# An attention and feed-forward kernel on one core: another order of instructions on four engines, and two PSUM banks shared by transposes and attention result

## The chip, the core and the metric

The kernel runs on 1 core of one Trainium2 chip. The metric is the device time of one execution in microseconds (us); shown is the median of several runs. One execution was also profiled, and all rows of the profile come from that one.

The engines are named as the profile names them: PE multiplies matrices (PEld is its loading of the stationary operand), DVE, ACT and POOL work on elements, SP issues DMAs. Each engine takes its instructions in the order in which they stand in its queue, and an instruction that waits holds up those behind it on the same engine. A line number such as L203 is that of the kernel before; in the changed kernel the same statements of the functions stand up to 7 lines lower.

## The reference

```python
# q, k, v: (8, 8, 576, 64) float32, tau = 0.02; w_in (512, 2048), w_out (2048, 512) float64
scores = 0.125 * np.matmul(q, k.transpose(0, 1, 3, 2))
thresh = np.max(scores, axis=-1, keepdims=True) - tau
scores = np.where(scores >= thresh, scores, -1000000000.0)
scores = scores - np.max(scores, axis=-1, keepdims=True)
attn = np.exp(scores)
attn = attn / (np.sum(attn, axis=-1, keepdims=True) + 1e-09)
x = np.matmul(attn, v)          # (8, 8, 576, 64)
x = x.transpose(0, 2, 1, 3).reshape(4608, 512)
h = x @ w_in
r = np.maximum(h, 0.0)
out = (r * r) @ w_out           # (4608, 512)
```

## The kernel before, in words

Two heads are taken together (32 pairs). Their 576 queries are cut into four blocks of 128 and a rest of 64; the rests of the two heads share a block. Work goes by *steps*, one block of a pair each, 160 in all (numbered from 0). The first four pairs are visited twice, first blocks 0, 1, 2 (steps 0 to 11), then blocks 3 and 4 (steps 12 to 19), so that the first chunk of the feed-forward part is ready early; from step 20 on each pair has its five blocks in one visit. Everything is issued by one loop over the steps, and its order of statements is the order in every queue: no scheduler moves anything.

A step does the following.

- `scores`: PE multiplies one block of queries with all keys (L179) into PSUM tiles s0 and s1, one for each head, two banks each and only one copy of them. DVE takes the row maximum (L183) and three small numbers from it: the bias b (L184), the threshold (L185) and z (L188). ACT takes the exponentials (L191).
- `threshold`: DVE sets to zero what lies under the threshold and sums the rest (L203); after it s0 and s1 are free for the next step's scores. Then the reciprocal of the sum (L205, L206), and POOL divides (L208).
- `turn`, for the step before, in three parts: PE transposes a third of the weights w (L220; L224, L230 and L231 for the block of rests) into a PSUM bank "tr", and ACT copies it to SBUF as wT (L221, L227, L232, L233). "tr" is one bank, so a part can't start before the copy of the part before has read it. Before step 13 (`early()`), parts 1 and 2 use the two "mm" banks, which the feed-forward part doesn't need yet.
- `mix`, two steps after the blocks 2 and 4 of a pair: PE multiplies wT with v (L247) into the bank "x", and ACT copies the result (L250) to xT.
- `fill`: what is waiting of the feed-forward part, in four portions between the parts of `turn`, by given costs of each piece of PE work. `mlp_in` multiplies xT with w_in (L263), ACT takes the relu (L267), POOL squares it (L269); `mlp_out` multiplies with w_out (L279), ACT copies (L283), SP stores. Chunks of 384 tokens are released at fixed steps: chunk 0 at step 13, the next at step 39.
- `load_qk`, `load_v`: SP loads the next pair. `prep`, at the end of the second step of a visit: DVE lays out qT and kT of the next pair (L154), POOL copies the pieces qmid (L161) and the first columns of kT (L157), which the next visit's first scores read.
- `round_weights`: the weights come as float64 and are rounded to float32 in 32 pieces, four of them loaded ahead. Stage 0 is two conversions on ACT (L113, L114), stage 1 three bit operations on DVE (L116, L117, L119), stage 2 a multiply and an addition on POOL (L121, L122). Their tile cv has two copies. A piece's stages 0, 1 and 2 stand after the scores, before the threshold, and at the end of its step. Pieces per step come from `FEW, MORE = 0.5, 1.6`: one in steps 1, 3, 5, 7, 9, 11 and 12; then 2, 1, 2, 2, 1, 2, 1 in steps 13 to 19; 2, 2, 1, 2, 1, 2, 2, 1 in steps 20 to 27; and the last in step 28.

PSUM's eight banks: s0 and s1 take four, "mm" two, "tr" one, "x" one.

Of the kernel before, what the change touches and what calls it, by code (L numbers as in the profile page):

```python
# [9 lines left out]
FP32 = mybir.dt.float32  # L10
U32 = mybir.dt.uint32
AF = mybir.ActivationFunctionType
ALU = mybir.AluOpType
# [6 lines left out]
def kernel(  # L20
# [75 lines left out]
    def load_weights(i):  # L96
        nc.sync.dma_start(out=weight_area(i).bitcast(mybir.dt.int64), in_=weight_piece(i)[0])
# [3 lines left out]
    def round_weights(i, stage):  # L101

        words = weight_area(i).bitcast(U32).rearrange("p (n w) -> p n w", w=2)
        lo, hi = words[:, :, 0], words[:, :, 1]
        if stage == 0:
            rounding[i] = pool.tile([P, 3, WP], FP32, tag="cv", name="cv")
        t, e, d = (rounding[i][:, x, :] for x in range(3))  # L110
        tu, eu = t.bitcast(U32), e.bitcast(U32)
        if stage == 0:
            nc.scalar.activation(out=e, in_=hi.bitcast(FP32), func=AF.Copy, scale=2.0 ** -112)  # L113
            nc.scalar.activation(out=d, in_=lo, func=AF.Copy, scale=2.0 ** -52)  # L114
        elif stage == 1:
            nc.vector.tensor_scalar(out=tu, in0=hi, scalar1=0x80000000, scalar2=None, op0=ALU.bitwise_and)  # L116
            nc.vector.scalar_tensor_tensor(out=tu, in0=eu, scalar=3, in1=tu, op0=ALU.logical_shift_left,  # L117
                                           op1=ALU.bitwise_or)
            nc.vector.tensor_scalar(out=eu, in0=tu, scalar1=0xFF800000, scalar2=None, op0=ALU.bitwise_and)  # L119
        else:  # L120
            nc.gpsimd.tensor_tensor(out=d, in0=d, in1=e, op=ALU.mult)  # L121
            nc.gpsimd.tensor_tensor(out=weight_piece(i)[1], in0=t, in1=d, op=ALU.add)  # L122

    loaded, ready = {}, {}
# [40 lines left out]
    def scores(vis, i):  # L165

        qT, kT = ready[vis]
        n = 2 if i < NBLK else 1
        sc = [psum.tile([P, 2, 512], FP32, tag=f"s{u}", name=f"s{u}") for u in range(n)]
        halves = [(half, u) for half in range(2) for u in range(n)]  # L170
        if early():
            halves.sort(key=lambda x: x[1])
        for half, u in halves:
            if i < NBLK:
                rows, lhsT = slice(u * D, (u + 1) * D), qT[u * D:(u + 1) * D, i * P:(i + 1) * P]
            else:
                rows, lhsT = slice(0, P), qmid[vis % 2]
            at = (0 if u else REST) + half * HALF
            nc.tensor.matmul(sc[u][:, half, 0:HALF], lhsT, kT[rows, at:at + HALF], start=True, stop=True)  # L179
        st = pool.tile([P, 7, 2], FP32, tag="st", name="st", bufs=4)  # L180
        mx, bias, thr, z = (st[:, j, 0:n] for j in range(4))
        for u in range(n):
            nc.vector.tensor_reduce(out=mx[:, u:u + 1], in_=sc[u][:, :, 0:HALF], axis=AX.XY, op=ALU.max)  # L183
        nc.vector.tensor_scalar(out=bias, in0=mx, scalar1=-SCALE, scalar2=None, op0=ALU.mult)  # L184
        nc.vector.tensor_scalar(out=thr, in0=mx, scalar1=ntau8, scalar2=None, op0=ALU.add)  # L185


        nc.vector.tensor_tensor(out=z, in0=thr, in1=mx, op=ALU.is_gt)  # L188
        w = pool.tile([P, n, S], FP32, tag="w", name="w", bufs=3)
        for u in range(n):  # L190
            nc.scalar.activation(out=w[:, u, :].rearrange("p (h k) -> p h k", h=2), in_=sc[u][:, :, 0:HALF],  # L191
                                 func=AF.Exp, bias=bias[:, u:u + 1], scale=SCALE)
        weights[vis, i] = w, sc, st

    def threshold(vis, i):


        w, sc, st = weights[vis, i]
        n = len(sc)
        mx, bias, thr, z, sm, den, rcp = (st[:, j, 0:n] for j in range(7))  # L200
        for u in range(n):
            wu = w[:, u, :].rearrange("p (h k) -> p h k", h=2)
            nc.vector.scalar_tensor_tensor(out=wu, in0=sc[u][:, :, 0:HALF], scalar=thr[:, u:u + 1], in1=wu,  # L203
                                           op0=ALU.is_ge, op1=ALU.mult, accum_out=sm[:, u:u + 1])
        nc.vector.scalar_tensor_tensor(out=den, in0=z, scalar=float(S), in1=sm, op0=ALU.mult, op1=ALU.add)  # L205
        nc.vector.reciprocal(rcp, den)  # L206
        for u in range(n):
            nc.gpsimd.tensor_scalar(out=w[:, u, :], in0=w[:, u, :], scalar1=z[:, u:u + 1],  # L208
                                    scalar2=rcp[:, u:u + 1], op0=ALU.add, op1=ALU.mult)

    def turn(vis, i, part):

        w = weights[vis, i][0]
        tag = "mm" if early() and part else "tr"
        ps = psum.tile([P, 4, P], FP32, tag=tag, name="w_ps", bufs=2 if tag == "mm" else 1)
        if i < NBLK:
            cols = slice(i * P, (i + 1) * P)
            for n in range(3):
                c = 3 * part + n
                nc.tensor.transpose(ps[:, n, :], w.rearrange("p u k -> p (u k)")[:, c * P:(c + 1) * P], ident)  # L220
            nc.scalar.copy(wT[:, 3 * part:3 * part + 3, cols], ps[:, 0:3, :])  # L221
        elif part == 0:
            for c in range(NBLK):
                nc.tensor.transpose(ps[:, c, :], w[:, 0, c * P:(c + 1) * P], ident)  # L224
            for u in range(2):
                at = u * (NBLK + 1)
                nc.scalar.copy(wT[:, at:at + NBLK, NBLK * P:S], ps[:, :, u * D:(u + 1) * D])  # L227
        elif part == 1:

            nc.tensor.transpose(ps[0:REST, 0, :], w[:, 0, S - REST:S], ident)  # L230
# [6 lines left out]
    def mix(n, cols):  # L237

        b, pr = divmod(visits[n][0], HP)
        if b // 2 not in xTs:  # L240
            xTs[b // 2] = pool.tile([P, NMC, 2 * S], FP32, tag="xT", name="xT")
        nq = cols.stop - cols.start
        ps = psum.tile([P, TCH], FP32, tag="x", name="x_ps")
        for c in range(NBLK + 1):
            for u in range(2):
                cw = NBLK if c == NBLK else u * (NBLK + 1) + c
                nc.tensor.matmul(ps[u * D:(u + 1) * D, 0:nq], vs[n % 2][:, u * (NBLK + 1) + c, :], wT[:, cw, cols],  # L247
                                 start=(c == 0), stop=(c == NBLK))
        to = (b % 2) * S + cols.start
        nc.scalar.copy(xTs[b // 2][:, pr, to:to + nq], ps[:, 0:nq])  # L250
# [64 lines left out]
    def early():  # L315
        return state["step"] < min(chunk_at)
# [20 lines left out]
            fn(*what)  # L337


    FEW, MORE = 0.5, 1.6  # L340
    at_once = min(chunk_at) - 2
    rounded = [min(n_pieces, int(FEW * (min(s, at_once) + 1) + MORE * max(s - at_once, 0))) for s in range(NST)]
    load_qk(0)
    load_v(0)
    for i in range(RAW):
        load_weights(i)
    for part in range(2):
        prep(0, part)
    for s in range(NST + 3):
        state["step"] = s  # L350
        now = range(rounded[s - 1] if s else 0, rounded[s]) if s < NST else ()
        if s < NST:
            n, i = steps[s]
            at = visits[n][1].index(i)
            if at == 0 and n + 1 < len(visits):
# [18 lines left out]
        if s < NST:  # L374
# [42 lines left out]
```

## Time and profile before

| | us |
|---|---|
| median of 3 runs | 1743.04 (1740.65 to 1743.19) |
| the profiled execution, its own time | 1741.98 |
| its span, first to last instruction | 1740.2 |
| PE busy | 1586.0 (91%) |
| DVE, ACT, POOL busy | 697.3, 565.8, 496.5 |
| granted PE clock, mean over the span | 0.968 |
| longest waits of PE: for the transposes' copies (L221), the thresholds (L203), the rests' copies (L227), kT's columns (L157) | 64.8, 30.4, 24.5, 16.2 |

Rows of the profile read like this. In a timeline: start, duration, engine, line, operation, out<-in, shape, how many such instructions in a row, and in brackets how long the engine stood idle before it and who released it. In a table of waits: engine and line that waited, for whom; total us, how often, the longest. In groups of instructions: busy time, mean ns of one, idle time before. A matmul of float32 shows as two records, so the eight records of one step's scores are four matmuls.

### The profile page before, as it was taken

Reading aid. Unit: us, or ns where it says so; the run is one execution under the profiler, and the core shown is the slowest. Engines: PE = TensorE matmul, PEld = TensorE weight load, DVE = VectorE, ACT = ScalarE, POOL = GpSimd, SP = SyncE. Lnnn points to the kernel's source line nnn. Section 1 sums busy time; section 2 is a strip of 40 time slices with the busy share of each in tenths; the row PEclk is TensorE's granted clock in tenths of the full one; section 3 lists DMA queues with packets and bytes.
Section 4 is the critical chain, followed back from the end, with each engine's and each line's share of the span. In section 5 each row is a group of like instructions: output and inputs, shape, how many; then the busy total and the mean of one; then the engine's idle time right before and its main releaser. Section 6 shows DMA issues by size and latency. Waiting matters only on the chain.

```text
span 1740.2 us, 18567 instructions
## 1 busy us (share of the span) xinstructions
PE 1586.0 (91%) x6464; PEld 853.6 (49%) x6464; DVE 697.3 (40%) x1833; ACT 565.8 (33%) x1157; POOL 496.5 (29%) x655
## 2 busy tenths in 40 slices
PE   5766677889999999999999999999999999999999
PEld 3433333445545545545545545545445545545453
DVE  5755676444334343434334333434333334430000
ACT  3443443333323333323323333333323323322010
POOL 3445465123213213223213213214223213213030
PEclk8778888999999999999999999999999999999999
DMA  5334331021021010111011011021012011000000
GB/s 127 78 90 111 91 86 45 7 53 21 6 49 26 7 41 12 25 35 21 21 31 30 6 36 18 15 43 23 15 31 35 1 33 27 0 26 1 13 6 18
DMA packets 224189, 59.28 MB, mean 34 GB/s; under 512 B 215392, under 2 KB 215392, under 8 KB 224096
## 3 DMA queue, kind: packets, MB, share of 16 engines
q1 hardware_dynamic: 224064, 58.10, 14.9%
q8 instruction: 51, 0.84, 0.2%
q14 instruction: 42, 0.34, 0.1%
q0 software_dynamic: 32, 0.00, 0.0%
HBM read 48.63 MB, written 9.44 MB: 33 GB/s over the span
## 4 chain that ended last, share of the span: by engine, by line
PE 79%; DVE 8%; ACT 7%; POOL 3%; issue 2%; SPq 0%; DMA 0%; ACTq 0%; DVEq 0%; POOLq 0%
PE o L279 27%; PE h L263 24%; PE s L179 11%; PE x_ps L247 9%; PE w_ps L220 7%; DVE st L183 5%; ACT w L191 3%; ACT wT L221 1%; DVE w L203 1%; POOL cv L121 1%; DVE cv L117 1%; DVE st L184 1%; ACT cv L113 1%; ACT wT L227 1%; POOL w_in_sb L122 1%
## 5 line engine op out<-in xcount | busy, mean ns | idle before, releaser
L263 PE MATMUL h<-xT,w_in_sb 128*128 128x384 f32 x1536 | 556.4, 498 | 0.0
L279 PE MATMUL o<-w_out_sb,g 128*128 128x512 f32 x1152 | 544.2, 602 | 0.0
L183 DVE TENSOR_REDUCE st<-s 128x1 f32<-128x576 f32 x288 | 207.2, 753 | 733.4 <-PE s L179 733.3
L208 POOL TENSOR_SCALAR w<-w,st 128x576 f32<-128x576 f32 x288 | 233.9, 821 | 663.6 <-DVE st L206 600.4
L191 ACT ACTIVATE w<-s,st 128x576 f32<-128x576 f32 x288 | 199.2, 737 | 552.0 <-DVE st L184 444.4
L263 PEld LDWEIGHTS h<-xT,w_in_sb 128*128 128x128 f32 x1536 | 274.7, 193 | 166.0 <-issue 35.3
L269 POOL TENSOR_TENSOR g<-r 128x384 f32<-128x384 f32 x192 | 159.2, 829 | 525.9 <-ACT r L267 525.7
L279 PEld LDWEIGHTS o<-w_out_sb,g 128*128 128x128 f32 x1152 | 202.2, 192 | 190.4 <-issue 189.1
L221 ACT COPY wT<-w_ps 128x384 f32<-128x384 f32 x384 | 181.4, 480 | 246.5 <-PE w_ps L220 246.3
L220 PEld LDWEIGHTS w_ps<-ident,w 128*128 128x128 f32 x1152 | 148.5, 146 | 221.5 <-issue 96.6
L220 PE MATMUL w_ps<-ident,w 128*128 128x128 f32 x1152 | 197.6, 286 | 65.2 <-ACT wT L221 64.8
L203 DVE SCALAR_TENSOR_TENSOR w<-s,st,w 128x576 f32<-128x576 f32 x288 | 225.0, 814 | 79.6 <-ACT w L191 79.6
L179 PE MATMUL s<-kT,qT 64*128 64x288 f32 x1024 | 184.6, 459 | 56.9 <-DVE w L203 27.4
L179 PEld LDWEIGHTS s<-kT,qT 64*128 64x128 f32 x1024 | 104.5, 200 | 146.1 <-issue 94.9
L247 PE MATMUL x_ps<-wT,vs 128*64 128x192 f32 (+1 forms) x1280 | 174.7, 421 | 0.0
L267 ACT ACTIVATE r<-h 128x384 f32<-128x384 f32 x192 | 94.4, 492 | 181.1 <-PE h L263 172.1
L247 PEld LDWEIGHTS x_ps<-wT,vs 128*64 128x64 f32 x1280 | 87.9, 140 | 81.2 <-issue 76.0
L283 ACT COPY osb<-o 128x512 f32<-128x512 f32 x36 | 21.1, 586 | 85.3 <-PE o L279 83.5
L250 ACT COPY xT<-x_ps 128x384 f32<-128x384 f32 (+1 forms) x64 | 25.4, 397 | 51.4 <-PE x_ps L247 51.4
L179 PE MATMUL s<-kT,qmid 128*128 128x288 f32 x128 | 38.4, 425 | 3.1 <-DVE w L203 3.1
L121 POOL TENSOR_TENSOR cv<-cv 128x512 f32<-128x512 f32 x32 | 40.5, 1267 | 0.0
L188 DVE TENSOR_TENSOR st<-st 128x2 f32<-128x2 f32 (+1 forms) x160 | 38.1, 238 | 5.5
(37 smaller groups left out, 505.4 us busy)
## 6 DMA issues: line engine op xcount, KB each, us to landing
ql<-in_q_dram SPq DMA_DIRECT2D x144, 72.0 KB, 2.5
kl<-in_k_dram SPq DMA_DIRECT2D x144, 72.0 KB, 2.6
vs<-in_v_dram SPq DMA_DIRECT2D x72, 128.0 KB, 2.4
out_dram<-osb SPq DMA_DIRECT2D x36, 256.0 KB, 2.1
area<-in_moe_w_in_dram SPq DMA_DIRECT2D x16, 512.0 KB, 3.9
area<-in_moe_w_out_dram SPq DMA_DIRECT2D x16, 512.0 KB, 3.6
vs<-in_v_dram SPq DMA_DIRECT2D x72, 16.0 KB, 2.2
ntau<-in_tau_dram POOLq DMA_DIRECT2D x1, 0.5 KB, 3.3
```

Of the source, the lines that this page charges most:

```text
L179: nc.tensor.matmul(sc[u][:, half, 0:HALF], lhsT, kT[rows, at:at + HALF], start=True, stop=True)
L183: nc.vector.tensor_reduce(out=mx[:, u:u + 1], in_=sc[u][:, :, 0:HALF], axis=AX.XY, op=ALU.max)
L191: nc.scalar.activation(out=w[:, u, :].rearrange("p (h k) -> p h k", h=2), in_=sc[u][:, :, 0:HALF], func=AF.Exp, bias=bias[:, u:u + 1], sca ...
L203: nc.vector.scalar_tensor_tensor(out=wu, in0=sc[u][:, :, 0:HALF], scalar=thr[:, u:u + 1], in1=wu, op0=ALU.is_ge, op1=ALU.mult, accum_out=s ...
L208: nc.gpsimd.tensor_scalar(out=w[:, u, :], in0=w[:, u, :], scalar1=z[:, u:u + 1], scalar2=rcp[:, u:u + 1], op0=ALU.add, op1=ALU.mult)
L220: nc.tensor.transpose(ps[:, n, :], w.rearrange("p u k -> p (u k)")[:, c * P:(c + 1) * P], ident)
L221: nc.scalar.copy(wT[:, 3 * part:3 * part + 3, cols], ps[:, 0:3, :])
L247: nc.tensor.matmul(ps[u * D:(u + 1) * D, 0:nq], vs[n % 2][:, u * (NBLK + 1) + c, :], wT[:, cw, cols], start=(c == 0), stop=(c == NBLK))
L263: nc.tensor.matmul(h, w_in_sb[:, c, f * P:(f + 1) * P], xT[:, c, at:at + TCH], start=(c == 0), stop=(c == NMC - 1))
L267: nc.scalar.activation(out=r, in_=h, func=AF.Relu)
L269: nc.gpsimd.tensor_tensor(out=gs[j, f], in0=r, in1=r, op=ALU.mult)
L279: nc.tensor.matmul(o, gs[j, f][:, t * P:(t + 1) * P], w_out_sb[:, f, :], start=(f == 0), stop=(f == NFT - 1))
```

## The change

- The pieces to be rounded are set by hand. Steps 0 to 11 have one piece, except for the second step of each visit, which has `prep`; steps 12 to 19 have one each, steps 20 to 27 two each.
- Rounding has four stages, the multiply (2) and the addition (3) on POOL now apart. The first piece's conversions stand ahead of the scores' part of a step (on ACT: ahead of the exponentials), its bit operations right behind the maximum and its small numbers, its multiply ahead of the division, its addition at the step's end. A second piece has all its stages at the end of the step.
- `exponents` and `divide` are functions of their own. In steps with a piece, and in the early ones, the exponentials stand where they stood; in all others they stand behind the copy of the first third of `turn`. `threshold` moves from behind part 1 to behind part 0, the division stands behind part 1.
- `prep` moves from the end of the second step of a visit to right behind its maximum, ahead of the threshold.
- "tr" and "x" are replaced by "tx" with two banks, which transposes and mix take in turn. Early, only part 1 still uses "mm".

```diff
+        elif stage == 2:
+            nc.gpsimd.tensor_tensor(out=d, in0=d, in1=e, op=ALU.mult)
         else:
-            nc.gpsimd.tensor_tensor(out=d, in0=d, in1=e, op=ALU.mult)
             nc.gpsimd.tensor_tensor(out=weight_piece(i)[1], in0=t, in1=d, op=ALU.add)
...
-        tag = "mm" if early() and part else "tr"
-        ps = psum.tile([P, 4, P], FP32, tag=tag, name="w_ps", bufs=2 if tag == "mm" else 1)
+        ps = psum.tile([P, 4, P], FP32, tag="mm" if early() and part == 1 else "tx", name="w_ps", bufs=2)
...
-        ps = psum.tile([P, TCH], FP32, tag="x", name="x_ps")
+        ps = psum.tile([P, TCH], FP32, tag="tx", name="x_ps", bufs=2)
...
+    for s, (n, i) in enumerate(steps):
+        if s <= min(chunk_at) - 2:
+            x = int(visits[n][1].index(i) != 1)
+        else:
+            x = 1 if n < 2 * HP else 2
...
+            if now:
+                round_weights(now[0], 0)
             scores(n, i)
-        for p in now:
-            round_weights(p, 0)
+            if now or early():
+                exponents(n, i)
+            if now:
+                round_weights(now[0], 1)
+                round_weights(now[0], 2)
+            if at == 1 and more:
+                prep(n + 1, 0)
+                prep(n + 1, 1)
...
             if 0 < s <= NST:
                 turn(*steps[s - 1], part)
-            if part == 1 and s < NST:
-                for p in now:
-                    round_weights(p, 1)
+            if on and part == 0:
+                if not (now or early()):
+                    exponents(n, i)
                 threshold(n, i)
+            if on and part == 1:
+                divide(n, i)
             fill(quarter)
-        if s < NST:
-            for p in now:
-                round_weights(p, 2)
-                if p + RAW < n_pieces:
-                    load_weights(p + RAW)
-            if n + 1 < len(visits):
-                if at == 1:
-                    prep(n + 1, 0)
-                    prep(n + 1, 1)
-                if at == len(visits[n][1]) - 1:
-                    load_v(n + 1)
+        if on:
+            if now:
+                end_rounding(now[0])
+            for p in now[1:]:
+                for stage in range(3):
+                    round_weights(p, stage)
+                end_rounding(p)
+            if more and at == len(visits[n][1]) - 1:
+                load_v(n + 1)
```

The order of PE's instructions is the same in both kernels. On POOL, in step 15 (the last block of a pair, whose next pair is laid out), before: the division, two pieces of weights, qmid and kT, a square, and the division of step 16.

```order
L208 TENSOR_SCALAR w<-w,st 128x576
L121 TENSOR_TENSOR cv<-cv 128x512
L122 TENSOR_TENSOR w_in_sb<-cv 128x512
L121 TENSOR_TENSOR cv<-cv 128x512
L122 TENSOR_TENSOR w_in_sb<-cv 128x512
L161 COPY qmid_79<-qT 64x64 x2
L157 COPY kT<-kT 64x64
```

And in the changed kernel, where L123 is the addition and L216 the division; the first addition belongs to step 14.

```order
L123 TENSOR_TENSOR w_in_sb<-cv 128x512
L121 TENSOR_TENSOR cv<-cv 128x512
L162 COPY qmid_79<-qT 64x64 x2
L158 COPY kT<-kT 64x64
L276 TENSOR_TENSOR g<-r 128x384
L216 TENSOR_SCALAR w<-w,st 128x576
```

The copy of kT moved ahead of the step's division and ahead of all but one of the instructions for weights.

On ACT, in step 15 before: the exponentials (of one tile, the rests), the conversions of two pieces, the copy of the mix, a relu and the three copies of the transposes.

```order
L191 ACTIVATE w<-s_894,st 128x576
L113 ACTIVATE cv<-area 128x512
L114 ACTIVATE cv<-area 128x512
L113 ACTIVATE cv<-area 128x512
L114 ACTIVATE cv<-area 128x512
L250 COPY xT<-x_ps 128x192
L267 ACTIVATE r<-h 128x384
L221 COPY wT<-w_ps 128x3x128 x3
```

And in the changed kernel (L196 the exponentials, L257 the mix's copy, L228 the transposes' copies).

```order
L113 ACTIVATE cv<-area 128x512
L114 ACTIVATE cv<-area 128x512
L196 ACTIVATE w<-s_906,st 128x576
L257 COPY xT<-x_ps 128x192
L274 ACTIVATE r<-h 128x384
L228 COPY wT<-w_ps 128x3x128 x3
```

The one piece's conversions now stand ahead of the exponentials, and none stands between them and the copies.

On ACT far from the rounding, in step 52 (the third block of a pair), before: exponentials, an output copy, then the copies of the transposes' thirds with relus between.

```order
L191 ACTIVATE w<-s_3110,st 128x576
L191 ACTIVATE w<-s_3111,st 128x576
L283 COPY osb<-o 128x512
L221 COPY wT<-w_ps 128x3x128 x2
L267 ACTIVATE r<-h 128x384
L221 COPY wT<-w_ps 128x3x128
```

And in the changed kernel, where L290 is the output copy.

```order
L290 COPY osb<-o 128x512
L228 COPY wT<-w_ps 128x3x128
L196 ACTIVATE w<-s_3110,st 128x576
L196 ACTIVATE w<-s_3111,st 128x576
L228 COPY wT<-w_ps 128x3x128
L274 ACTIVATE r<-h 128x384
L228 COPY wT<-w_ps 128x3x128
```

The output copy and the first third's copy moved ahead of the exponentials.

More of the change, by code (lines that the diff above doesn't have):

```diff
@@ L189, in scores, with exponents @@
         w = pool.tile([P, n, S], FP32, tag="w", name="w", bufs=3)
-        for u in range(n):
+        weights[vis, i] = w, sc, st
+    def exponents(vis, i):
+        w, sc, st = weights[vis, i]
+        for u in range(len(sc)):
             nc.scalar.activation(out=w[:, u, :].rearrange("p (h k) -> p h k", h=2), in_=sc[u][:, :, 0:HALF],
-                                 func=AF.Exp, bias=bias[:, u:u + 1], scale=SCALE)
-        weights[vis, i] = w, sc, st
+                                 func=AF.Exp, bias=st[:, 1, u:u + 1], scale=SCALE)
     def threshold(vis, i):
@@ L206, in threshold, with divide @@
         nc.vector.reciprocal(rcp, den)
-        for u in range(n):
+    def divide(vis, i):
+        w, sc, st = weights[vis, i]
+        z, rcp = st[:, 3, :], st[:, 6, :]
+        for u in range(len(sc)):
             nc.gpsimd.tensor_scalar(out=w[:, u, :], in0=w[:, u, :], scalar1=z[:, u:u + 1],
@@ L337, in fill, with end_rounding @@
             fn(*what)
-    FEW, MORE = 0.5, 1.6
-    at_once = min(chunk_at) - 2
-    rounded = [min(n_pieces, int(FEW * (min(s, at_once) + 1) + MORE * max(s - at_once, 0))) for s in range(NST)]
+    pieces, left = [], n_pieces
+    for s, (n, i) in enumerate(steps):
[3 more added lines that the diff above has]
+            x = 1 if n < 2 * HP else 2
+        pieces.append(min(x, left))
+        left -= pieces[-1]
+    assert left == 0
+    def end_rounding(p):
+        round_weights(p, 3)
+        if p + RAW < n_pieces:
+            load_weights(p + RAW)
     load_qk(0)
@@ L348 @@
         prep(0, part)
+    done = 0
     for s in range(NST + 3):
         state["step"] = s
-        now = range(rounded[s - 1] if s else 0, rounded[s]) if s < NST else ()
-        if s < NST:
+        on = s < NST
+        now = []
+        if on:
             n, i = steps[s]
             at = visits[n][1].index(i)
-            if at == 0 and n + 1 < len(visits):
+            now = list(range(done, done + pieces[s]))
+            done += pieces[s]
+            more = n + 1 < len(visits)
+            if at == 0 and more:
                 load_qk(n + 1)
+            if now:
+                round_weights(now[0], 0)
             scores(n, i)
-        for p in now:
-            round_weights(p, 0)
+            if now or early():
[6 more added lines that the diff above has]
+                prep(n + 1, 1)
         if s in mixes:
@@ L368 @@
                 turn(*steps[s - 1], part)
[L369 to L371 removed]
+            if on and part == 0:
+                if not (now or early()):
+                    exponents(n, i)
                 threshold(n, i)
+            if on and part == 1:
+                divide(n, i)
             fill(quarter)
[L374 to L384 removed]
+        if on:
+            if now:
[6 more added lines that the diff above has]
+                load_v(n + 1)
 _INS = ['q', 'k', 'v', 'tau', 'moe_w_in', 'moe_w_out']
```

## The prediction

> **What bounds the kernel now.** I read the page first, then the busy time cut by stretch, then PE's waits by stretch, then the rows of single steps. The first page lines say that PE is the engine with by far the most work.
>
> ```profile
> span 1740.2 us, 18567 instructions
> PE 1586.0 (91%) x6464; PEld 853.6 (49%) x6464; DVE 697.3 (40%) x1833; ACT 565.8 (33%) x1157; POOL 496.5 (29%) x655
> ```
>
> I cut the span where the row maximum (L183) of steps 0, 13, 20, 28 and 39 starts. Columns: the stretch, its length, then busy time of PE, weight load, DVE, ACT, POOL, the granted clock, DMA. I call the five rows A to E; E is 121 steps.
>
> ```profile
> 11.00:107.60 96.60, 65.76 (x271) 41.41 (x270) 70.70 (x172) 42.16 (x80) 36.81 (x44) 0.77 0.42 98
> 107.60:199.30 91.70, 59.62 (x246) 33.63 (x246) 51.23 (x106) 32.49 (x68) 48.39 (x55) 0.83 0.42 102
> 199.30:292.50 93.20, 66.12 (x265) 35.51 (x265) 66.32 (x128) 39.59 (x78) 53.84 (x55) 0.85 0.28 76
> 292.50:382.70 90.20, 75.32 (x331) 38.43 (x333) 43.07 (x122) 32.01 (x64) 19.92 (x28) 0.96 0.07 16
> 382.70:1566.50 1183.80, 1147.37 (x4866) 615.10 (x4868) 463.84 (x1299) 397.33 (x820) 307.10 (x429) 1.00 0.12 24
> ```
>
> PE idles 31 us in A, 32 in B, 27 in C, 15 in D, 36 in E. What it waits for there, in the same order (the first row belongs to A):
>
> ```profile
> PE s L179 <- DVE w L203: 30.4, 10, 4.6
> ...
> PE s L179 <- POOL kT L157: 16.2, 4, 6.2
> PE w_ps L220 <- ACT wT L221: 8.7, 4, 3.3
> PE s L179 <- DVE kT L154: 4.7, 3, 2.8
> ...
> PE w_ps L220 <- ACT wT L221: 22.0, 9, 5.3
> PE w_ps L230 <- ACT wT L227: 5.1, 2, 4.1
> ...
> PE w_ps L220 <- ACT wT L221: 11.6, 11, 2.5
> PE w_ps L230 <- ACT wT L227: 3.3, 2, 1.9
> ...
> PE w_ps L220 <- ACT wT L221: 22.5, 27, 1.4
> PE w_ps L230 <- ACT wT L227: 13.6, 13, 1.4
> ```
>
> So A waits for the thresholds, which free the scores' banks; B for the little copy of kT on POOL; C, D and E for the copy that frees the one bank of the transposes. These are the only places where time can be won: PE's own order is the same instruction for instruction in both kernels, and so is the number of instructions on every engine.
>
> **The change part by part.** *A, steps 0 to 12.* One step with a weight piece, before:
>
> ```profile
> 15.76 2.99 PE L179 MATMUL s<-kT,qT 64*128 64x288 f32 x8 [4.40 <-DVE w L203]
> 18.05 1.49 DVE L183 TENSOR_REDUCE st<-s 128x1 f32<-128x576 f32 x2 [1.31 <-PE s L179]
> ...
> 19.84 1.37 ACT L191 ACTIVATE w<-s,st 128x576 f32<-128x576 f32 x2 [4.46 <-DVE st L184]
> ...
> 19.99 0.42 DVE L116 TENSOR_SCALAR cv<-area 128x512 uint32<-128x512 uint32 x1
> ...
> 21.79 0.69 DVE L117 SCALAR_TENSOR_TENSOR cv<-cv 128x512 uint32<-128x512 uint32 x1 [1.38 <-ACT cv L113]
> ...
> 22.52 0.43 DVE L119 TENSOR_SCALAR cv<-cv 128x512 uint32<-128x512 uint32 x1
> 22.86 0.81 DVE L203 SCALAR_TENSOR_TENSOR w<-s,st,w 128x576 f32<-128x576 f32 x1
> ...
> 23.83 2.99 PE L179 MATMUL s<-kT,qT 64*128 64x288 f32 x8 [2.96 <-DVE w L203]
> ```
>
> The step takes 23.83 - 15.76 = 8.07 us, and 1.38 of it is DVE waiting for the two conversions, which stand behind the exponentials on ACT. With the conversions ahead, that wait goes and the three bit operations (0.42 + 0.69 + 0.43 = 1.54) run beside the exponentials: such a step is 8.07 - 1.3 = about 6.8. Seven steps have a piece before; the step with a mix among them is bound by PE's own row, so six win 1.3 each, -7.8. But the change puts pieces, or the two transposes of the next heads, into steps that had nothing between maximum and threshold: there the 1.54 comes in where the threshold waited only about 0.7 (one of the two exponentials) anyway, so +0.85 in three steps, +2.6. The first exponential now stands behind two conversions that need the first piece from DRAM, +0.5, and for z and the bit operations held up now and then by POOL (below) I add 0.7: -4. Bounds: +4 (the new work is not covered at all, three more steps at 1.5) and -13 (PE stays warm: the eight score matmuls take 2.99 cold here, and 1.24 in the row below, and about nine steps could win 1.05 each on the part ahead of the first maximum).
>
> *B, steps 13 to 19.* The worst place, from a step with the last block to the next pair of heads:
>
> ```profile
> 141.97 0.74 DVE L154 STREAM_TRANSPOSE kT<-kl 128x576 f32<-128x576 f32 x1
> ...
> 143.55 1.26 POOL L122 TENSOR_TENSOR w_in_sb<-cv 128x512 f32<-128x512 f32 x1
> ...
> 147.78 0.24 POOL L157 COPY kT<-kT 64x64 f32<-64x64 f32 x1
> ```
>
> kT is laid out at 142.7, its copy starts at 147.8: four POOL instructions of two pieces stand between. In the change one multiply stands ahead of the copy, and the layout comes before the threshold; the copy is then done while PE still has the mix, the fill and nine transposes to do. The 16.2 goes, and what is late next is PE itself. The 4.7 goes with it, since the layout is earlier. The 8.7 and what is left go because the conversions no longer stand between exponential and copy, and because a second bank lets the next transposes start. Two queues are passed. On POOL the division now waits for the multiply (1.27, row in C), and behind it PE's transposes, but those come only after the next step's scores and a fill. On SP the loads keep their places, one piece at a time where two or three stood, asked for four pieces ahead; no row of PE's waits names one. On ACT the conversions open a step, and if a piece were late the exponentials would stand behind it: four pieces are four steps here, and no engine's wait before names a load of weights. PE has 59.6 us of work there, part of it at half speed (clock 0.83). I take 61: -31. Bounds: -20 (12 us of new waits) and -40 (no wait, and cold matmuls warm up to about 52).
>
> *C, steps 20 to 27.* The change rounds two pieces in each of the eight steps, 16 in all, where 13 stood. This speaks against the gain: POOL and DVE stop each other.
>
> ```profile
> 134.40 1.15 DVE L188 TENSOR_TENSOR st<-st 128x1 f32<-128x1 f32 x1
> ...
> 135.61 1.40 POOL L122 TENSOR_TENSOR w_in_sb<-cv 128x512 f32<-128x512 f32 x1
> ...
> 135.99 1.57 DVE L117 SCALAR_TENSOR_TENSOR cv<-cv 128x512 uint32<-128x512 uint32 x1
> ...
> L117 DVE SCALAR_TENSOR_TENSOR cv<-cv x32: 691/693/1579, 21.8 to 296.2; 128x512 uint32<-128x512 uint32 x32
> ```
>
> L117 takes 0.69 alone and 1.57 when a POOL addition runs beside it; it ends 0.55 after that addition. If they never overlap, the stretch needs, with these rows,
>
> ```profile
> L121 POOL TENSOR_TENSOR cv<-cv 128x512 f32<-128x512 f32 x32 | 40.5, 1267 | 0.0
> L208 POOL TENSOR_SCALAR w<-w,st 128x576 f32<-128x576 f32 x288 | 233.9, 821 | 663.6 <-DVE st L206 600.4
> L269 POOL TENSOR_TENSOR g<-r 128x384 f32<-128x384 f32 x192 | 159.2, 829 | 525.9 <-ACT r L267 525.7
> ```
>
> 16 x 2 x 1.267 = 40.5, 15 divisions x 0.82 = 12.3, some 7 squares x 0.83 = 5.8, and 16 x 1.54 = 24.6 on DVE: 83 us, with the small ones 85. If they overlap as they please, PE's own 66.1 bounds it. I take the row's side, 85: -8. Bounds: 0 (a wait besides) and -25. The Trainium skill has the rule, on "SBUF — State Buffer", section "Who interferes with whom": a DVE instruction with two SBUF inputs, or one in a two-port mode, shares a port pair with GpSimd, and the loser is blocked for the whole instruction. The trace agrees (0.69 against 1.57); by the rule to the letter the stretch is the 85 that I take.
>
> *D and E, steps 28 to 159.* The transposes and the mix now take turns in two banks, the thirds of a step no longer wait for each other's copy, and on ACT the copy of the first third goes ahead of the exponentials:
>
> ```profile
> 452.09 1.24 PE L179 MATMUL s<-kT,qT 64*128 64x288 f32 x8
> ...
> 513.72 0.58 ACT L283 COPY osb<-o 128x512 f32<-128x512 f32 x1
> 514.18 0.50 ACT L221 COPY wT<-w_ps 128x384 f32<-128x384 f32 x1
> 514.73 0.55 PE L220 MATMUL w_ps<-ident,w 128*128 128x128 f32 x3 [0.52 <-ACT wT L221]
> 515.12 1.46 PE L263 MATMUL h<-xT,w_in_sb 128*128 128x384 f32 x4
> ```
>
> A bank is needed again two allocations later, with at least one fill of 1.46 between, against a copy of 0.50. Of E's 36.1 I take back 30, of D's 14.9 10 (fills are thin there, some steps will wait for the threshold instead). Bounds: D -4 to -14; E -12 (a third, if the mix's copy now holds the second third) to -36. The exponentials move later; how much room they have is the second rival. The stretch after E is untouched.
>
> **Sum**: -4 - 31 - 8 - 10 - 30 = -83 us, against the profiled execution's 1741.98 (span 1740.2 and 1.8 around it), which is 1.06 under the median: 1659.
>
> **Rivals.** *The port decides wherever pieces are rounded.* For it: the rows of L117, and L188's 1.15 on two numbers a partition; against it: in B POOL was busy 48 of 92 us with more pieces than it will have. Then A +4, B -18, C +8, D -6, E -28: -40, 1702.
>
> *The exponentials come too late (slower).* Outside the rounding they now wait behind the transposes of the step before, and the next scores wait for the threshold. From the end of the first transposes: copy 0.50, exponentials 1.37, second threshold 0.81, hand-overs about 0.6: 3.3, or 4.3 with an output copy (0.58) and a relu between. PE meanwhile has three fills of 1.46 and two transposes of 0.5: 5.4. Against it, therefore, 1.1 to 2.1 us of room; for it, only that ACT's queue was not seen in this order. It makes the whole slower when the tail is over 6.2: A to D win 53, E's idle 36 is gone, and 121 x 0.76 eats both and 3.5 more. With a tail of 6.4, -89 + 121 = +32: 1774.
>
> *Sharing only renames the wait.* The second third waits for the mix's copy, or the first for the last; E wins nothing: -53, 1689. For it: 40 waits of about 0.9 in E, each only a little beyond its cover. Against it: two allocations apart instead of one.
>
> *PE warms up as well.* The clock is 0.77, 0.83 and 0.85 in A, B and C; if filled gaps bring it to 1.0, then A -12, B -38, C -22, D -13, E -34: -119, 1623. The Trainium skill, "TensorE: Matmul & The Clock Gate", section "What's actually happening", says that PE runs at half rate until it has been busy for one window of some 3.4 us; by that rule A, which still pauses in each step, stays cold and only B and C gain, which is within my bounds. The rows agree in the factor: 2.99 against 1.24.
>
> **How the numbers follow.** Forecast 0.63, port 0.09, late exponentials 0.05, renamed wait 0.10, warm PE 0.13. The range takes in the renamed wait and the warm PE and the bounds of B, C and E, but not the port's 1702: 1622 to 1697 (all bounds of the terms at once, which I don't expect, would be 1614 to 1710). Within 0.2% (3.5 us, about what a measurement of this kernel can tell from none) needs two rivals at once: 0.02. Faster 0.93, slower 0.05.
>
> **What would show it.** Right: no wait of PE for the kT copy; waits of L220's successor for ACT under 10 us over the span; B near 61 us, E near 1154; C with POOL and DVE busy in turn, near 85. Wrong: score matmuls in E that wait for the threshold (late exponentials); L117's successors at 1.5 us throughout and A longer than 97 us (port); E at 1184 (renamed wait); A under 88 us at a clock over 0.9 (warm PE).

## The result, and the profile after

The changed kernel takes 1625.33 us (median of 4 runs, 1624.97 to 1627.12) against 1743.12 of the kernel before, timed beside it: a ratio of 0.9328, 95% interval 0.9312 to 0.9345. The prediction said 1659, within 1622 to 1697. The profiled execution took 1627.12, with a span of 1625.4; that is 114.9 less than the profiled execution before, where the prediction's sum was -83.

The first lines of the page after: PE's instructions are as many, its share has risen to 96%.

```profile
span 1625.4 us, 18644 instructions
PE 1561.2 (96%) x6464; PEld 851.8 (52%) x6464; DVE 696.0 (43%) x1833; ACT 556.3 (34%) x1157; POOL 503.6 (31%) x655
```

The same five stretches, cut where the row maximum (now L184) of the same steps starts; columns as before (length, busy time of PE, weight load, DVE, ACT, POOL, then the granted clock).

```profile
10.90:101.90 91.00, 64.51 (x272) 40.26 (x270) 70.05 (x178) 44.36 (x85) 43.25 (x49) 0.86 0.51 116
101.90:151.90 50.00, 47.50 (x248) 28.71 (x247) 41.29 (x94) 27.48 (x60) 36.70 (x45) 0.98 0.63 139
151.90:234.90 83.00, 64.22 (x266) 35.79 (x265) 78.17 (x137) 40.86 (x82) 62.71 (x61) 0.88 0.41 103
234.90:313.10 78.20, 74.58 (x331) 39.33 (x329) 43.68 (x120) 29.73 (x62) 19.79 (x27) 0.98 0.09 19
313.10:1451.50 1138.40, 1138.40 (x4865) 618.16 (x4866) 459.95 (x1298) 389.83 (x819) 310.74 (x431) 1.00 0.12 25
```

In the last row PE's busy time is the whole stretch. PE's waits by stretch, A to D in order; in E there is no row at all.

```profile
PE s L180 <- DVE w L207: 26.4, 10, 4.2
...
PE s L180 <- DVE w L207: 2.3, 3, 0.9
PE s L180 <- POOL kT L158: 0.2, 1, 0.2
...
PE w_ps L227 <- ACT wT L228: 10.3, 3, 4.1
PE s L180 <- DVE w L207: 4.9, 3, 4.2
PE w_ps L227 <- ACT xT L257: 3.2, 1, 3.2
...
PE s L180 <- DVE w L207: 3.4, 3, 2.0
```

The wait for kT went from 16.2 to 0.2, those for the transposes' copies in E from 36.1 to none. What is left is A, where PE still waits for the thresholds, and C. There the transposes wait 13.5 us for ACT (10.3 and 3.2), above the 10 that the prediction gave as a sign. From here on a stretch runs from the start of the maximum of its first step to that of the next stretch's first step; E then ends with the maximum of step 159. (The prediction's row of E ran 2.6 us further.) Each stretch is read from one profiled execution of its kernel.

| us | A | B | C | D | E |
|---|---|---|---|---|---|
| before | 96.7 | 91.7 | 93.2 | 90.2 | 1181.2 |
| after | 91.0 | 50.0 | 83.0 | 78.2 | 1135.9 |
| measured | -5.7 | -41.7 | -10.1 | -12.0 | -45.3 |
| predicted | -4 | -31 | -8 | -10 | -30 |

### The profile page after: what moved, and what is told of

The parts are those of the page before. It is cut to its first block, busy times and chain, and to the rows that moved or that the text cites. A ratio compares the mean times of both kernels' runs of the same rounds, so it can differ in the third digit from the quotient of the medians.

```text
span 1625.4 us, 18644 instructions
## 1 busy us (share of the span) xinstructions
PE 1561.2 (96%) x6464; PEld 851.8 (52%) x6464; DVE 696.0 (43%) x1833; ACT 556.3 (34%) x1157; POOL 503.6 (31%) x655
## 4 chain that ended last, share of the span: by engine, by line
PE 89%; DVE 7%; SPq 1%; issue 1%; ACT 0%; POOL 0%; DMA 0%; DVEq 0%; ACTq 0%; POOLq 0%
PE o L286 30%; PE h L270 29%; PE s L180 11%; PE x_ps L254 10%; PE w_ps L227 7%; DVE st L184 2%; DVE w L207 2%; DVE cv L117 1%; PE w_ps L231 1%; SPq L136 1%; DVE cv L119 1%; DVE cv L116 1%; DVE st L185 1%; DVE st L186 0%; ACT w L196 0%
## 5 line engine op out<-in xcount | busy, mean ns | idle before, releaser
L270 PE MATMUL h<-xT,w_in_sb 128*128 128x384 f32 x1536 | 549.7, 493 | 0.0
L216 POOL TENSOR_SCALAR w<-w,st 128x576 f32<-128x576 f32 x288 | 238.0, 835 | 565.8 <-DVE st L210 550.2
L184 DVE TENSOR_REDUCE st<-s 128x1 f32<-128x576 f32 x288 | 206.8, 753 | 417.8 <-PE s L180 417.8
L207 DVE SCALAR_TENSOR_TENSOR w<-s,st,w 128x576 f32<-128x576 f32 x288 | 224.8, 814 | 315.9 <-ACT w L196 315.8
L228 ACT COPY wT<-w_ps 128x384 f32<-128x384 f32 x384 | 180.8, 482 | 316.4 <-PE w_ps L227 315.4
L196 ACT ACTIVATE w<-s,st 128x576 f32<-128x576 f32 x288 | 200.2, 745 | 56.7 <-DVE st L185 56.6
L227 PE MATMUL w_ps<-ident,w 128*128 128x128 f32 x1152 | 189.2, 282 | 14.1 <-ACT wT L228 10.3
L254 PEld LDWEIGHTS x_ps<-wT,vs 128*64 128x64 f32 x1280 | 89.1, 142 | 82.9 <-issue 70.7
L257 ACT COPY xT<-x_ps 128x384 f32<-128x384 f32 (+1 forms) x64 | 25.4, 397 | 242.2 <-PE x_ps L254 242.2
L290 ACT COPY osb<-o 128x512 f32<-128x512 f32 x36 | 21.1, 586 | 104.0 <-PE o L286 101.8
L186 DVE TENSOR_SCALAR st<-st,ntau 128x2 f32<-128x2 f32 (+1 forms) x160 | 39.4, 246 | 0.0
```

What stands on the lines that cost most here:

```text
L270: nc.tensor.matmul(h, w_in_sb[:, c, f * P:(f + 1) * P], xT[:, c, at:at + TCH], start=(c == 0), stop=(c == NMC - 1))
```

## The experiments

The kernels below are the kernel before with one part of the change, or the changed kernel with one part taken back. Four parts were tried so: the banks, the late exponentials with the earlier threshold, the early layout and the stages of rounding; the numbers of pieces per step were not tried alone. In the kernels the parts stand behind switches, and the code below shows only the statements that matter, without the switches. Line numbers differ by a few; the tile and the operation tell what a row is. Each kernel was timed beside the kernel before. Stretches of all of them:

| us | time | ratio to before, interval | A | B | C | D | E |
|---|---|---|---|---|---|---|---|
| shared banks alone | 1675.17 | 0.9615, 0.9600 to 0.9629 | 96.5 | 90.4 | 84.9 | 78.9 | 1135.9 |
| late exponentials alone | 1678.33 | 0.9633, 0.9617 to 0.9649 | 88.7 | 83.2 | 90.9 | 84.0 | 1143.2 |
| early layout alone | 1722.14 | 0.9883, 0.9867 to 0.9900 | 96.7 | 70.9 | 93.7 | 90.1 | 1181.3 |
| rounding stages alone | 1713.96 | 0.9833, 0.9818 to 0.9848 | 87.5 | 81.2 | 84.1 | 89.1 | 1181.2 |
| change, banks taken back | 1643.25 | 0.9432, 0.9418 to 0.9446 | 89.4 | 52.9 | 86.7 | 80.8 | 1143.2 |
| change, late exponentials taken back | 1625.51 | 0.9332, 0.9318 to 0.9346 | 93.1 | 50.0 | 83.0 | 75.8 | 1135.9 |
| change, early layout taken back | 1638.28 | 0.9403, 0.9389 to 0.9417 | 91.6 | 64.7 | 83.3 | 76.0 | 1135.9 |
| change, three copies of cv | 1627.11 | 0.9335, 0.9321 to 0.9349 | 89.7 | 49.9 | 83.1 | 78.2 | 1135.9 |
| change, multiply on DVE | 1630.60 | 0.9350, 0.9336 to 0.9364 | 91.3 | 49.9 | 87.4 | 77.0 | 1135.9 |
| change, three pieces earlier | 1621.45 | 0.9301, 0.9286 to 0.9317 | 92.3 | 50.6 | 78.1 | 75.3 | 1135.9 |
| the same, the rest spread | 1617.21 | 0.9274, 0.9260 to 0.9287 | 93.5 | 49.8 | 68.1 | 79.5 | 1135.9 |
| change, little work on POOL | 1609.45 (one run) | | 91.9 | 49.9 | 67.5 | 75.2 | 1135.9 |

**E: banks or order?** The prediction gave E's win to both. Four kernels take them apart. First the banks alone:

```diff
-        ps = psum.tile([P, 4, P], FP32, tag=tag, name="w_ps", bufs=2 if tag == "mm" else 1)
+        ps = psum.tile([P, 4, P], FP32, tag="mm" if early() and part == 1 else "tx", name="w_ps", bufs=2)
...
-        ps = psum.tile([P, TCH], FP32, tag="x", name="x_ps")
+        ps = psum.tile([P, TCH], FP32, tag="tx", name="x_ps", bufs=2)
```

> The kernel before with one part of the change: transposes and mix share two PSUM banks; all orders as before. The stretch from step 39 to the last step (E) took 1183.8 us before and 1138.4 in the change. If the second bank ends E's waits, or if either of the two parts is enough: E 1137 to 1142, time 1665 to 1685 (D and C win some too). If the place of the first third's copy on ACT, ahead of the exponentials, ends them: E 1170 or more, time 1710 to 1730.

Then the order alone:

```diff
+            if on and part == 0:
+                if not (now or early()):
+                    exponents(n, i)
+                threshold(n, i)
             if on and part == 1:
                 for p in now:
                     round_weights(p, 1)
-                threshold(n, i)
+                divide(n, i)
```

> The kernel before with one part of the change: outside rounding and the early steps the exponentials stand behind the copy of the first third, the threshold behind part 0, the division behind part 1; one bank for the transposes and one for the mix as before. If the second bank ends E's waits: E 1175 to 1184, time 1730 to 1743. If the order on ACT ends them, or either part is enough: E 1137 to 1145, time 1685 to 1700.

And the changed kernel with the one or the other taken back by the same lines:

> The changed kernel with one bank for the transposes and one for the mix again. If the second bank ends E's waits: E 1165 to 1180 where the change has 1138.4, time 1652 to 1668. If the order on ACT ends them or either is enough: E 1138 to 1143, time 1626 to 1640 (the stretches with rounding may lose some).

> The changed kernel with the exponentials always right behind the maximum's small numbers and the threshold behind part 1. If the order on ACT ends E's waits: E 1165 to 1180, time 1652 to 1668. If the second bank ends them or either is enough: E 1138 to 1143, time 1625 to 1632.

Measured: either is nearly enough. With the banks alone E is 1135.9, as in the change; with the order alone it is 1143.2, and nine waits are left, the same as with the banks taken back from the change. PE's row of waits in E with the order alone, and E's own row:

```profile
PE w_ps L233 <- ACT wT L234: 5.3, 9, 0.6
...
357.80:1503.40 1145.60, 1140.31 (x4864) 617.65 (x4866) 459.68 (x1298) 390.03 (x819) 307.47 (x430) 1.00 0.12 25
```

So the order of ACT adds nothing to the banks in E, and in the whole nothing either: taken back, the time is 1625.51. In A, B and C it can't matter, since every step there is an early one or has a piece: the changed kernel and the one with this part taken back have the same instructions in the same order on every engine. A still took 91.0 in the one and 93.1 in the other; the granted clock was 0.86 and 0.74:

```profile
11.10:104.20 93.10, 65.88 (x271) 41.01 (x272) 69.02 (x178) 44.35 (x85) 43.32 (x49) 0.74 0.51 114
```

So differences of about 2 us in A are differences between executions. From step 28 on the order does differ, and D is 2.4 shorter with it taken back. But D moves as much with what C leaves over (75.2 to 78.2 in the kernels of the table that have the change's order there), so it stays open whether the late exponentials cost anything in D. By itself this part won more than either theory had (1678 against 1685 and over). In A and B all that it moves is the threshold, on DVE now ahead of the bit operations, and A is 8.0 shorter and B 8.5. With the banks taken back 1643 is over the range, as B, C and D lose 9.2 together.

**B: the copy of kT, or the conversions?** The layout alone, moved as in the change, then the stages of rounding alone (with the pieces per step of before), then the change with the layout at the step's end again.

```diff
             scores(n, i)
+            if at == 1 and more:
+                prep(n + 1, 0)
+                prep(n + 1, 1)
```

> The kernel before with one part of the change: the next heads are laid out right behind the maximum and its small numbers, not at the end of the step. If the late copy of kT is what B (steps 13 to 19, 91.7 us before) loses most by: B 68 to 76, time 1718 to 1728. If the conversions in ACT's queue are, and the wait for kT is only late for another reason: B 84 or more, time over 1732.

```diff
+            if now:
+                round_weights(now[0], 0)
             scores(n, i)
+            exponents(n, i)
+            if now:
+                round_weights(now[0], 1)
+                round_weights(now[0], 2)
```

> The kernel before with one part of the change: the first piece's conversions ahead of the exponentials, its bit operations behind the maximum, its multiply ahead of the division, its addition at the end; pieces per step, layout and banks as before. If the late copy of kT is what B loses most by: B 78 to 88 (the copy still stands behind an addition or two pieces), time 1720 to 1735. If the conversions are: B 60 to 72. A (96.7 before): 90 to 93 if the conversions ahead of the exponentials are what the change wins there.

> The changed kernel with the next heads laid out at the end of the step again. If the late copy of kT is what B lost most by: B 60 to 68 where the change has 50.0, time 1636 to 1646. If the conversions are: B 50 to 54, time under 1632.

The layout alone takes 20.8 us off B, just what PE waited there for kT (16.2 + 4.7); the stages alone take 10.5. The layout taken back from the change costs 14.7 in B. So the late copy was the largest loss, as the prediction has it, but not the only one. (The stages' time, 1714, is below its range of 1720 to 1735, and A, 87.5, below its 90 to 93: A and C are 9 shorter each.) PE's waits in B with the layout alone:

```profile
PE w_ps L243 <- ACT wT L240: 9.7, 3, 4.0
PE w_ps L233 <- ACT wT L234: 4.5, 4, 2.1
PE s L182 <- DVE w L209: 0.7, 2, 0.4
```

No wait for kT is left; those for the copies, which stand behind conversions on ACT, grew from 11.2 to 14.2. And with the stages alone:

```profile
PE s L182 <- DVE kT L157: 13.0, 4, 4.7
PE w_ps L233 <- ACT wT L234: 4.1, 4, 1.6
PE s L182 <- POOL kT L160: 3.5, 4, 1.4
```

There the copies' waits fall to 4.1, and kT is waited for on DVE, since its layout still stands at the step's end. Each part removes its own wait. The change has both, one piece in each of these steps instead of up to two, and the shared banks; 2.5 us of waits are left there. What the smaller number of pieces gives wasn't tried apart.

**C: what makes a step with two pieces up to 12 us long?** The longest wait of all in C after is this one, of ACT:

```profile
ACT cv L113 <- POOL w_out_sb L123: 29.8, 7, 5.3
```

A conversion waits for the addition that frees its tile, and the exponentials stand behind it. The prediction holds that POOL and DVE stop each other. In the first experiment cv has three copies for the parts that the addition reads:

```diff
-            rounding[i] = pool.tile([P, 3, WP], FP32, tag="cv", name="cv")
-        t, e, d = (rounding[i][:, x, :] for x in range(3))
+            rounding[i] = (pool.tile([P, 2, WP], FP32, tag="cv", name="cv", bufs=3),
+                           pool.tile([P, WP], FP32, tag="cve", name="cve", bufs=2))
+        t, d = (rounding[i][0][:, x, :] for x in range(2))
+        e = rounding[i][1]
```

> The changed kernel with three copies of the tile that a piece's addition frees (cv split in two, the part that the multiply frees with two copies), so that no conversion waits for the addition two pieces back. In C (steps 20 to 27, 83.0 us in the change) ACT waits 29.8 us for that. If POOL and DVE stopping each other sets C: C 80 to 84, time 1621 to 1626. If the conversions' wait for the tile sets it, with the exponentials behind them: C 68 to 75, time 1611 to 1618.

C stays at 83.1. The wait is gone from the table, and another of the same size stands there, of the exponentials for DVE:

```profile
ACT w L200 <- DVE st L189: 29.6, 8, 5.5
```

So the late tile cost nothing. Next, the multiply of each piece moves from POOL to DVE from step 20 on, which makes the sum of both engines smaller:

```diff
-            nc.gpsimd.tensor_tensor(out=d, in0=d, in1=e, op=ALU.mult)
+            on_dve = state["step"] >= 20
+            (nc.vector if on_dve else nc.gpsimd).tensor_tensor(out=d, in0=d, in1=e, op=ALU.mult)
```

> The changed kernel with the multiply of each piece on DVE instead of POOL from step 20 on. If POOL and DVE stop each other in C (83.0 us in the change), what counts is the sum of both: 16 multiplies of 1.27 become 16 of about 0.7, so C 72 to 77, time 1615 to 1620. If DVE's own queue sets C (it shows 78 of 83 us busy there), the 11 us more on DVE make it longer: C 85 to 94, time 1627 to 1637.

C grew to 87.4, though POOL was busy for 47.1 us instead of 62.7: neither that sum nor POOL's own queue is what counts. The groups of DVE show what does. In C of the change (count, busy, mean ns):

```profile
L117 DVE SCALAR_TENSOR_TENSOR cv<-cv 128x512 uint32<-128x512 uint32 x16 | 15.2, 949 | 3.1 <-ACT cv L113 1.6
L116 DVE TENSOR_SCALAR cv<-area 128x512 uint32<-128x512 uint32 x16 | 12.6, 787 | 0.0
...
L119 DVE TENSOR_SCALAR cv<-cv 128x512 uint32<-128x512 uint32 x16 | 11.4, 711 | 0.5
L184 DVE TENSOR_REDUCE st<-s 128x1 f32<-128x576 f32 x15 | 10.6, 742 | 0.9 <-PE s L180 0.9
L186 DVE TENSOR_SCALAR st<-st,ntau 128x2 f32<-128x2 f32 x7 | 6.0, 850 | 0.0
L185 DVE TENSOR_SCALAR st<-st 128x2 f32<-128x2 f32 x7 | 3.6, 520 | 0.2
```

The idle times in the last columns are small: DVE nearly always has something to run. But much of that is being held: L116 took 405 ns at its shortest in this execution, so 16 x (787 - 405) = 6.1 us of its 12.6 are not work. In the same way, with the shortest of its kind in the execution as the own work of each instruction of C, and what it took beyond that as held:

| DVE in C, us | own work | held | sum | C |
|---|---|---|---|---|
| change | 57.9 | 26.1 | 84.0 | 83.0 |
| three copies of cv | 57.9 | 26.3 | 84.2 | 83.1 |
| multiply on DVE | 68.9 | 17.5 | 86.4 | 87.4 |
| three pieces earlier | 53.2 | 23.5 | 76.7 | 78.1 |
| little work on POOL | 57.9 | 7.6 | 65.5 | 67.5 |

In these five kernels C lies within 2 us of DVE's own work and holds together. In the change, POOL was at work beside every instruction of DVE held by more than 0.06 us, 25.0 us in all: 16.8 beside additions and multiplies, 6.6 beside divisions, 1.6 beside squares. Not every kernel is so: with the layout taken back the sum is 79.3 and C 83.3, with the banks taken back 80.5 and 86.7; there DVE also waits, 9.2 and 10.1 us, for scores and conversions. One place shows how a hold looks, first DVE, then POOL, in step 22 of the change:

```profile
174.06 1.32 DVE L186 TENSOR_SCALAR st<-st,ntau 128x2 f32<-128x2 f32 x1
175.41 0.16 DVE L189 TENSOR_TENSOR st<-st 128x2 f32<-128x2 f32 x1
175.49 1.50 DVE L116 TENSOR_SCALAR cv<-area 128x512 uint32<-128x512 uint32 x1
...
174.09 1.27 POOL L121 TENSOR_TENSOR cv<-cv 128x512 f32<-128x512 f32 x1
175.44 1.27 POOL L123 TENSOR_TENSOR w_out_sb<-cv 128x512 f32<-128x512 f32 x1
```

L186 works on two numbers per partition and ends at 175.38, when POOL's multiply ends (175.36); the next starts between two POOL instructions and takes 0.16; L116 ends 0.28 after POOL's addition.

The last two rows of the table are from experiments of their own. In the one, three pieces move from C into A:

```diff
-            x = int(visits[n][1].index(i) != 1)
+            x = int(s != 1)
```

> The changed kernel with three more pieces early, one each in steps 4, 7 and 10, which have a mix and the layout of the next heads and are bound by PE's own row; 13 pieces are left for C. If the port's sum sets C, it falls by 3 x (2 x 1.27 + 1.54) = 12: C 70 to 73; A (91.0) grows by 1 to 4: time 1615 to 1620. If C is set by its chain of steps and not by the sum, it falls by less than 6 and the time stays over 1621.

C lost 4.9 and D 2.9, far from the 12 of the sum, while A and B grew by 1.9: the second expectation, with a time of 1621.45 just over its 1621. A piece less takes 1.6 us of DVE's own work and 0.9 of holds from C, not 4. In the other, POOL's work on the pieces nearly goes, and with it most of the holds:

```diff
-            nc.gpsimd.tensor_tensor(out=d, in0=d, in1=e, op=ALU.mult)
+            n = 8 if i >= n_in else WP
+            nc.gpsimd.tensor_tensor(out=d[:, 0:n], in0=d[:, 0:n], in1=e[:, 0:n], op=ALU.mult)
```

> The changed kernel, but of the 16 pieces of w_out POOL multiplies and adds only 8 of 512 columns (the rest of w_out stays zero from a memset at the start, so this kernel leaves out most of the rounding of w_out); DVE's and ACT's work is as in the change. In C of the change DVE's instructions take 57.9 us at their shortest, and 26.1 more held up beside POOL: 84 of 83. If the holds are what makes C longer than PE's work: held 3 to 8 us, C 63 to 69. If DVE's own chain of steps sets C and the holds only fill waits: C 76 or more. A starts some 6 to 9 us later for the memset, which is not counted.

The addition is shortened in the same way, and w_out starts as zeros. C falls to 67.5 with DVE's and ACT's work unchanged; POOL is busy for 31.8 us instead of 62.7. This kernel alone can't tell the holds from POOL's own work, but the multiply on DVE can: there too POOL did less, and C grew with DVE's work. (The memset costs nothing: the first maximum starts at 11.1 us, in the change at 11.0.) The row of C, and the groups of DVE there:

```profile
152.80:220.30 67.50, 57.81 (x267) 33.04 (x268) 59.74 (x137) 41.26 (x83) 31.83 (x61) 0.95 0.49 127
...
L120 DVE SCALAR_TENSOR_TENSOR cv<-cv 128x512 uint32<-128x512 uint32 x16 | 13.9, 867 | 6.0 <-ACT cv L116 4.6
...
L122 DVE TENSOR_SCALAR cv<-cv 128x512 uint32<-128x512 uint32 x16 | 10.4, 651 | 0.5
...
L119 DVE TENSOR_SCALAR cv<-area 128x512 uint32<-128x512 uint32 x16 | 6.8, 423 | 0.0
L191 DVE TENSOR_SCALAR st<-st,ntau 128x2 f32<-128x2 f32 x7 | 1.5, 220 | 0.0
```

The first bit operation is back at 423 ns, the threshold's small number at 220. The other two are still held, beside the divisions (6.2 of the 7.6 us), which this kernel leaves on POOL.

**A version that beats the change too.** With three pieces earlier and the 13 left spread over steps 20 to 29, two at a time only in steps 21, 24 and 29:

```diff
-            x = 1 if n < 2 * HP else 2
+            x = 2 if n >= 2 * HP and i in (1, NBLK) and s != 26 else 1
```

> As the kernel with three more pieces early, and the 13 pieces left are spread over steps 20 to 29, two in steps 21, 24 and 29 (which have a mix, so that PE has most to do), one in the others. If a step with one piece is bound by PE and one with two by the port where PE has no mix: C and D together (161.2 us in the change) 144 to 149, time 1610 to 1616. If the pieces cost the same wherever they stand: C and D 149 to 153.

C and D together took 147.6, in the first range, and the time is 1617.21, 1 over its range (the profiled execution took 1615.94, within it); its ratio's interval ends below the change's (0.9287 against 0.9312). In its row of C DVE is busy for 59 of 68 us, and the granted clock is 0.97 where the change has 0.88.

```profile
154.40:222.60 68.20, 56.48 (x265) 31.71 (x264) 58.84 (x120) 35.31 (x72) 46.91 (x50) 0.97 0.43 101
```

## Why the prediction was right in direction and 34 us too slow

Right: PE's order is the same, so the win is PE's lost time; its waits are where the prediction put them, and they went. What failed are sizes, in two terms above all.

*E, predicted -30, measured -45.3, past its own bound of -36.* The step "Of E's 36.1 I take back 30" counted only the idle rows and left 6 of them standing. No wait was left. And a wait costs PE more than its row: before, 40 waits with 36.1 us made E 45.3 longer than in the change, and with the order alone 9 waits with 5.3 us made it 7.3 longer. That is 0.23 and 0.22 us for each wait beyond its idle time. One place shows where that can come from. In the rows of the change, step 52:

```profile
440.66 1.46 PE L270 MATMUL h<-xT,w_in_sb 128*128 128x384 f32 x4
441.95 0.49 PE L227 MATMUL w_ps<-ident,w 128*128 128x128 f32 x3
442.28 1.46 PE L270 MATMUL h<-xT,w_in_sb 128*128 128x384 f32 x4
```

The transposes start 0.17 before the matmuls ahead of them end, and take 0.49; after the wait in step 52 before, they took 0.55 and overlapped nothing. In this place 0.17 + 0.06 is the 0.23; the other waits weren't taken apart. The second rival, the late exponentials, did not happen: E has no wait for a threshold. Nor did the renamed wait.

*B, predicted -31, measured -41.7, just past the bound of -40.* The waits fell as said, from 32.1 to 2.5. The step "I take 61" kept PE's own work near 59.6; it fell to 47.5, since the granted clock went from 0.83 to 0.98. That is what the rival of the warm PE has for B (-38), but not for the rest: C stayed at 0.88, and A's 0.86 is one execution's, with the same order in A also 0.74. That the measured 1625 lies near this rival's 1623 is luck: it has 18 us more than measured from A and C, and 11 less from E. The Trainium skill, "TensorE: Matmul & The Clock Gate", section "What's actually happening", has PE at half rate until one window of some 3.4 us was busy. B fits that (0.98 with 2.5 us of waits), and so does C of the spread version (0.97, with PE idle for 11.7 of 68 us instead of 18.8 of 83).

*C, predicted -8, measured -10.1.* The number was right by luck, for the step behind it was not. I added POOL's and DVE's durations as if the two together were one queue. In the change the runs show DVE's queue alone as the bound, its own 57.9 us and 26.1 of holds; moving work from POOL to DVE, which lowers that sum, made C longer. "SBUF — State Buffer", section "Who interferes with whom", in the Trainium skill, is borne out in that L117, with two SBUF inputs, is held and the threshold L207, with one input in PSUM, is not (0.77 to 0.82 throughout), and in that a hold lasts to the end of the other's instruction (1.32 us for two numbers a partition); the sum I drew from it was mine.

*A and D.* A won 5.7 and D 12.0, against 4 and 10, within their bounds. In A the stages alone gave 87.5 at an unchanged clock (0.76, before 0.77), 9.2 less than before, so the term of -7.8 for the conversions fits within the 2 us between executions; the threshold ahead of the bit operations gave 88.7. Both have seven pieces there. The change has nine, and gives some of this back. The layouts ahead of the thresholds are not the reason: A is 91.6 with them taken back, and with them alone 96.7, as before. The two more pieces may be; they weren't tried alone.

## What to carry to other kernels

When PE's order stays the same, sum its waits by stretch, and add for each of them the overlap that PE loses at a restart, and the clock that comes back when gaps close. Two cures for one wait (another bank, another order) don't add up: try each alone before keeping both. Before reading a stretch of one execution, compare it with kernels that have the same order there. And where POOL and DVE run side by side, read DVE's means against its shortest instructions: an engine that shows as busy may for a third of that be held (here 26.1 of 84.0 us).

## What the runs showed of the hardware that was not expected

- Each wait of PE for a copy cost 0.22 to 0.23 us beyond its idle row, as a mean of 9 and of 40 waits, here of float32 transposes of 128x128.
- The granted clock of one stretch differs between executions of the same order: 0.74 and 0.86 in A, where PE pauses in most steps.
- DVE's instructions on two numbers per partition were held by POOL as the long ones were: L186 took 222 ns as the median of its 160 and 1327 at most, while the thresholds on PSUM (L207) stayed at 807 ns in the mean in C.
- A 29.8 us wait in the table of waits was worth nothing: with its cause removed, another wait of 29.6 stood in its place and the stretch was 83.1 against 83.0.
